# Experts' numbers cast on VectorE, each unit's weight loads listed whole, and the order behind the first stage searched anew

## The chip, the cores and the metric

The kernel runs on one core of one Trainium2 chip. The metric is the device time of one execution in microseconds (us), from launch to the last output. The core has five engines with a queue of instructions each: TensorE (PE; its weight loads are shown as PEld), VectorE (DVE), ScalarE (ACT), GpSimd (POOL) and SyncE (SP, which here only issues DMA transfers and reads registers). Each engine takes its instructions strictly in the order in which they are listed, and waits at each one until what it needs is there.

## The reference

Three layers follow each other, all in float32:

```
attention   q, k, v [4, 8, 768, 64]; chunks of 32 queries see 8 memory keys and 56 keys around them
            out[:, :, chunk] = softmax(q_c k_full^T / 8) v_full         -> x [3072, 512]
first MLP   h = x @ w_in [512, 2048];  g = h * tanh(softplus(h));  y = g @ w_out [2048, 512]
MoE         logits = normalized(y) @ normalized(expert_emb [8, 512]).T / tau
            expert_idx = argmax(logits);  gate_w = softmax(logits)[expert_idx]
            for e in 8:  out[rows of e] = gate_w * (relu(y[rows of e] @ w1[e]) @ w2[e])
                         w1[e] [512, 1024], w2[e] [1024, 512]
```

## The kernel before

**Stages.** The 24 pairs of attention blocks run first and beside the first MLP. The MLP is cut into 8 blocks of 384 rows and 16 slices of 128 of the 2048 columns: 128 steps. A step is 12 matmuls into `p_h` (L732), a chain of elementwise work that goes to and fro between ScalarE and VectorE (tanh, square, exp, `rn` on ScalarE; `m` L751 on VectorE; a square L755 on ScalarE; L758, L761 on VectorE; the cast `gh` L334; `gl` L769 on VectorE), and 9 matmuls into `p_y` (L778). Every float32 operand is split into a high and a low part, so that three matmuls stand for one.

**MoE.** Rows are sorted by expert into slots of 128 rows. A *unit* is one or two slots of one expert: units 0 to 2 (two slots each) come from the first 21 row tiles ("group 1" of the routing), units 3 to 15 (pairs and singles) need all 24 tiles ("group 2"). For each unit GpSimd gathers its rows (`vn`, L1288), TensorE turns them (`p_xT`, L1331), then come the matmuls with `w1` (`p_h`, L1395 for two slots, L1429 for one) and with `w2` (`p_y`, L1485), a scaled copy `yo` (L1505, L1507) and a scatter by GpSimd (L1511). The expert's weights, 4 MB, come in eight transfers `eraw` of 512 KB (L1314), issued by SyncE into one of two sets of buffers; each piece is split into `ehi` (a cast, L334) and `elo` (a difference, L1367) before TensorE can use it.

**Routing.** In each group TensorE first counts (L1035/L1036 in group 1, L1061 in group 2), VectorE works out from the counts each row's place and each unit's expert `ef` (L1144 to L1146) and whether it differs from that of two units before, `ci` (L1152, L1153), TensorE makes the table of row numbers `p_tab` (L1218), and VectorE copies it (L1230) and makes `gi` (L1232), by which GpSimd gathers. `ei` is `ef` as whole numbers: a cast of at most 20 numbers in one partition (L1175). SyncE reads a unit's expert from `ei` into a register before that unit's first weight load:

```
if c == 0 and second == 0:
    tl["ev", u] = nc.sync.value_load(ei[0:1, x:x + 1], min_val=0, max_val=NE - 1)
```

So no weight of a unit can be loaded before its group's cast L1175 is done. That cast was given to GpSimd, behind the group's first two gathers.

**What sets the order.** All work is put down as jobs with the engines that may do them, a cost in ns, a rank and the jobs they come after. `Plan.order()` goes through a planned time and gives each engine the ready job of lowest rank; the order that comes out is what is listed. A job's rank gets a correction from the table `NUDGE`, one number for each kind of job and stretch of the program, found by search. The chip sees only the order.

Of the kernel before, what the change touches and what calls it, by code (L numbers as in the profile page):

```python
# [86 lines left out]
def between(a, b):  # L87
# [12 lines left out]


NUDGE = dict(
    acta0=-0.6, acta1=-1.74, acta2=50.36, actb0=-1.76, actb1=-96.54, actb2=-81.79, actb3=-42.59, att00=40.88,
    att01=6.03, att02=-14.41, att03=12.63, att04=-3.12, att05=6.33, att06=-6.99, att07=-18.03, att10=10.46, att11=7.93,
    att12=-2.03, att13=-0.28, att14=-5.39, att15=28.34, att16=0.19, att17=-11.65, att20=7.04, att21=-2.49, att22=6.84,
    att23=0.68, att25=11.02, att26=-13.24, att27=2.06, att30=-0.41, att31=-70.31, att32=-0.58, att33=-1.39,
    att35=-0.38, att36=-1.67, att37=-67.52, att40=0.45, att41=-0.43, att42=13.06, att43=-2.17, att44=-38.4,
    att45=12.86, att46=9, att47=-2.37, att50=-1.08, att51=-18.11, att52=-6.46, att53=252.42, att54=-0.22, att55=-3.21,
    att56=-1.09, att57=2.56, att60=-5.29, att61=2.16, att63=-69, att64=-3.49, att65=145.06, att66=-0.33, att67=-14.14,
    att70=-0.37, att71=-329.92, att72=0.25, att73=-193.55, att74=-10.54, att75=-2.18, att76=-1.27, e00=-1.37, e01=8.52,  # L110
    e10=3.1, e11=23.17, e20=-86.99, e21=1, e30=0.07, e31=1.64, e40=10.43, e41=28.57, e50=1.56, e51=-2.1, e60=-22.39,
    e61=17.86, e70=-0.44, e71=-5.41, em=3.37, en0=24.71, en1=-0.52, en2=4.38, en3=27.95, en4=-27.14, en5=-7.94,
    hh0=0.33, hh1=-9.8, hh2=7.9, ld00=-15.25, ld01=24.83, ld10=34.53, ld11=33.12, load0=8.15, load1=17.34, load10=5.31,
    load2=-45.54, load3=-3.15, load4=-2.18, load5=-0.64, load7=3.07, load9=4.58, mm_y0=20.47, mm_y1=14.69, mm_y2=275.2,
    mm_y3=-0.5, out0False=-95.98, out0True=2.61, out1False=4.84, out2False=6.58, raw0=-8.26, raw1=5.15, raw10=24.34,
    raw11=134.61, raw2=-9.44, raw3=-3.37, raw4=-0.07, raw5=-13.38, raw6=29.5, raw7=26.79, raw9=-0.21, route=3.96,
    rows0=21.85, rows1=0.04, rows2=2.04, split0=0.59, split10=130.91, split11=-16.93, split3=-2.85, split4=-6.67,
    split5=17.18, split6=34, split9=27.54, xs0=0.9, xs1=0.33, xs2=-187.61, ye0=0.64, ye1=82.2, ye2=137.26, ye3=-2.03,
    ye4=8.94, ye5=-5.92, yre0=-32.64, yre1=-4.26, yre3=-2.85, yre4=22.58, yre5=-10.72,
)  # L120
ATT = dict(q=0, k1=0, k2=0, Tq=1, Tk=1, qT=1, kT=1, v=2, mem=2, mem0=2, S=3, mx=3, ex=4, rg=5, rc=5, norm=5, PT=6, pT=6, V=7, xh=7, xl=7)

# [1 line left out]
def part(key):  # L124

    if key[0] == "issue":
        key = key[1:]
    n = key[0]
    x = key[1] if len(key) > 1 and isinstance(key[1], int) else 0
    if n in ATT:  # L130
        return f"att{x if x < 3 else min(x // 3, 5) + 2}{ATT[n]}"
    if n == "load":
        return f"load{x if x < 8 else 8 + x // 8}"
    if n in ("sign", "bias", "high", "low"):
        return f"raw{x if x < 8 else 8 + x // 8}"
    if n in ("hi", "lo"):
        return f"split{x if x < 8 else 8 + x // 8}"
    if n == "mm_y":
        return f"mm_y{0 if x < 4 else 1 if x < 24 else 2 if x < 48 else 3}"
    if n in ("tanh", "sq", "exp", "rn", "m"):  # L140
        return f"acta{0 if x < 4 else 1 if x < 24 else 2 if x < 48 else 3}"
    if n in ("m2", "rr", "g", "gh", "gl"):
        return f"actb{0 if x < 4 else 1 if x < 24 else 2 if x < 48 else 3}"
    if n in ("yT", "yb1", "yr1", "yb2", "yb3", "yL", "yL2", "ysq"):
        return f"rows{0 if x < 6 else 1 if x < 21 else 2}"
    if n in ("yout", "ystore", "y0out", "y0store", "y0load"):
        return f"out{0 if x < 6 else 1 if x < 21 else 2}{n[1] == '0'}"
    if n in ("shi", "slo"):
        return f"e{min(x, 6) if x < 6 else 6 + x % 2}{key[2]}"
    if n in ("hhi", "hlo", "relu", "hT"):  # L150
        return f"hh{0 if x < 6 else 1 + x % 2}"
    if n in ("xT", "xsh", "xsl"):
        return f"xs{0 if x < 6 else 1 + x % 2}"
    if n == "ld":
        return f"ld{0 if x < 2 else 1}{key[2]}"
    if n in ("ye", "yre", "en"):
        return f"{n}{x}"
    if n == "em":
        return "em"
    if n in ("r", "ids", "cnt", "tab"):  # L160
        return "route"
    return None


class Plan:
# [5 lines left out]
    def job(self, key, fn, on, rank, after=(), get=(), use=(), lat=130, tiled=False, dmas=0):  # L171
        uses = list(use) + [h for _, h in get]
        for h in uses:
            self.users.setdefault(h, []).append(key)
        for _, h in get:
            self.getter[h] = key
        self.jobs[key] = dict(fn=fn, on=on, rank=rank + NUDGE.get(part(key), 0), after=list(after), get=list(get), use=list(use), lat=lat, tiled=tiled, dmas=dmas,
                              need=[(tag, sum(t == tag for t, _ in get)) for tag in dict(get)])
# [102 lines left out]
def attn_moe_moe_kernel(ctx, tc, q, k, v, mem_k, mem_v, w_in, w_out, emb, tau, w1, w2, cst, out, ydbg=None):  # L281
    nc = tc.nc
# [30 lines left out]
    job, A, V_, G, E = plan.job, "Activation", "DVE", "Pool", "PE"  # L313
# [603 lines left out]
    ef, ei, ci = const.tile([1, NUNIT], F32, name="ef"), const.tile([1, NUNIT], I32, name="ei"), const.tile([1, NUNIT], I32, name="ci")  # L917
# [10 lines left out]
    def routing():  # L928
# [8 lines left out]
        rank = {1: KFF * NBLK - 12, 2: KFF * NBLK - 9}  # L937
# [42 lines left out]
        def group(g):  # L980
            i0, i1 = (0, T1) if g == 1 else (T1, NTILE)
            n = i1 - i0
            S8, c = [128, n, NE], slice(i0, i1)
# [3 lines left out]
            rk = rank[g]  # L987
# [169 lines left out]
            if g == 1:  # L1157
                ex = steps(experts(0, u1, evens[1], "e1") + change(2, 0, u1 - 2), [k3], rk)
# [12 lines left out]
            first = 0 if g == 1 else u1  # L1171

            def numbers(e):
                c = slice(first, u1 if g == 1 else NUNIT)
                nc.gpsimd.tensor_copy(ei[:, c], ef[:, c])  # L1175

            job(("experts", g), numbers, {G: 200}, rank=rk, after=[ex] + [("issue", "gather", first, a) for a in range(2)])


            CH = 3 if g == 2 else CH1  # L1180
# [74 lines left out]

        plan.group = group
        group(1)
        group(2)

    NC_ = 4
# [4 lines left out]
    def unit(u, base, x, cols, main=True, after=0, then=0):  # L1267
# [3 lines left out]
        g = 1 if x < FIRST // 2 else 2  # L1271
# [4 lines left out]
        def put_job(key, fn, on, rank, after=(), get=(), use=(), dma=None):  # L1276
            if not main:
                fn(next(iter(on)))
            elif dma:
                plan.dma(key, fn, on, dma, rank, after, get, use)  # L1280
            else:
                job(key, fn, on, rank, after, get, use)
# [16 lines left out]
        def load(second, c):  # L1299
            def f(e):  # L1300
                if c == 0 and second == 0:
                    tl["ev", u] = nc.sync.value_load(ei[0:1, x:x + 1], min_val=0, max_val=NE - 1)
                    if main and u >= 2:
                        tl["cv", u] = nc.sync.value_load(ci[0:1, x:x + 1], min_val=0, max_val=1)
                if u < 2:
                    raw[b, second, c] = wp.tile([128, 1024], F32, tag=f"w{8 * b + 4 * second + c}", name="eraw")
                kw = dict(cond=tl["cv", u]) if main and u >= 2 else {}
                if second:
                    src = w2[bass.ds(tl["ev", u], 1), c * 256:(c + 1) * 256, :].rearrange("a (k p) f -> p (a k) f", p=128)
                    dst = raw[b, second, c].rearrange("p (k f) -> p k f", k=2)  # L1310
                else:
                    src = w1[bass.ds(tl["ev", u], 1), :, c * FC:(c + 1) * FC].rearrange("a (k p) f -> p (a k) f", p=128)
                    dst = raw[b, second, c].rearrange("p (k f) -> p k f", k=KDM)
                nc.sync.dma_start(out=dst, in_=src, **kw)  # L1314
            return f

        for second in range(2):
            for c in range(NC_):
                h = ("eraw", b, second, c)
                after = [("experts", g)] + ([("slo", u - 2, second, c)] if u >= 2 else [])  # L1320
                if c or second:
                    after.append(("issue", "ld", u, second, c - 1) if c else ("issue", "ld", u, 0, NC_ - 1))
                put_job(("ld", u, second, c), load(second, c), dict(SP=470), base - 7 + 1.5 * second + 0.3 * c, after,
                        [(f"w{8 * b + 4 * second + c}", h)] if u < 2 else [], [] if u < 2 else [h], dma=2 ** 19)


# [168 lines left out]
        for n in range(2 * NC_ if split_y else 0):  # L1495
            c = n % NC_
# [23 lines left out]
    def late(n, x, cols):  # L1520
        unit(FIRST // 2 + MAIN_P + MAIN_S + n, 0, x, cols, False)
# [70 lines left out]
    for kind, n in TURNS:  # L1592
        c = FIRST + 2 * n
        todo.append((FIRST // 2 + n, [c, c + 1]) if kind == "P" else (FIRST // 2 + PAIRS + n, [FIRST + 2 * PAIRS + n]))
    base = KFF * NBLK
# [51 lines left out]
```

## Time and profile before

| what | us |
|---|---|
| median of 3 runs (lowest, highest) | 1021.76 (1020.55, 1022.34) |
| the profiled execution's own time | 1021.15 |
| its span, first to last instruction | 1019.4 |
| TensorE busy | 991.5 (97%) |
| VectorE, ScalarE, GpSimd busy | 809.0, 648.8, 189.5 |
| mean granted TensorE clock | 0.991 of full speed |

TensorE is busy for 97% of the span, so the table says which engine bounds the kernel and how little idle time there is to take away, some 28 us. It does not say where that time lies, nor what is lost where TensorE is busy at a lower clock. Both are read from the stretches and waits that are shown below.

### The profile page before, as it was taken

Reading aid. Unit: us, or ns where it says so; the run is one execution under the profiler, and the core shown is the slowest. Engines: PE = TensorE matmul, PEld = TensorE weight load, DVE = VectorE, ACT = ScalarE, POOL = GpSimd, SP = SyncE. Lnnn points to the kernel's source line nnn. Section 1 sums busy time; section 2 is a strip of 40 time slices with the busy share of each in tenths; the row PEclk is TensorE's granted clock in tenths of the full one; section 3 lists DMA queues with packets and bytes.
Section 4 is the critical chain, followed back from the end, with each engine's and each line's share of the span. In section 5 each row is a group of like instructions: output and inputs, shape, how many; then the busy total and the mean of one; then the engine's idle time right before and its main releaser. Section 6 shows DMA issues by size and latency. Waiting matters only on the chain.

```text
span 1019.4 us, 22817 instructions
## 1 busy us (share of the span) xinstructions
PE 991.5 (97%) x8575; PEld 879.2 (86%) x8575; DVE 809.0 (79%) x1799; ACT 648.8 (64%) x1534; POOL 189.5 (19%) x142
## 2 busy tenths in 40 slices
PE   7899999999999999999999999999989999999997
PEld 6678888898888888888888899888979988988986
DVE  4889999669899869769869867979948667777972
ACT  4788888776877777778777767757424334443431
POOL 5000100000000000000000000011136455555742
PEclk9989999999999999999999999999989999999999
DMA  9997661233645234325313100089089868467300
GB/s 181 253 237 200 168 184 45 59 128 97 184 132 135 74 78 134 84 46 145 84 25 122 30 20 20 1 272 327 32 279 371 280 229 296 150 218 246 127 29 23
DMA packets 171817, 146.36 MB, mean 144 GB/s; under 512 B 105114, under 2 KB 134410, under 8 KB 171444
## 3 DMA queue, kind: packets, MB, share of 16 engines
q1 hardware_dynamic: 164868, 128.53, 43.5%
q0 software_dynamic: 5104, 15.89, 4.6%
q8 instruction: 69, 1.13, 0.5%
q10 hardware_dynamic: 1728, 0.43, 0.3%
q14 instruction: 48, 0.39, 0.1%
HBM read 137.11 MB, written 16.53 MB: 151 GB/s over the span
## 4 chain that ended last, share of the span: by engine, by line
PE 76%; DVE 8%; DMA 7%; issue 5%; POOL 2%; SPq 1%; ACT 0%; POOLq 0%; DVEq 0%
PE p_h L732 23%; PE p_y L778 23%; PE p_y L1485 10%; PE p_h L1395 9%; DMA eraw<-in_moe_w_dram 2%; PE p_h L1429 2%; DMA kn<-in_k_dram 2%; PE p_X L621 2%; PE p_S L559 2%; POOL elo L1367 1%; SPq L319 1%; PE p_PT L602 1%; PE p_xT L1331 1%; PE p_qT L511 1%; DMA qn<-in_q_dram 1%
## 5 line engine op out<-in xcount | busy, mean ns | idle before, releaser
L732 PE MATMUL p_h<-xt,win_h 128*128 128x384 f32 x1024 | 268.9, 344 | 0.6 <-DVE rn L761 0.5
L732 PEld LDWEIGHTS p_h<-xt,win_h 128*128 128x128 f32 x1024 | 185.3, 191 | 10.2 <-DVE rn L761 1.8
L732 PE MATMUL p_h<-xt,win_l 128*128 128x384 f32 x512 | 173.9, 340 | 0.0
L334 ACT CAST ehi<-eraw 128x1024 fp32r<-128x1024 f32 x89 | 92.9, 1049 | 120.0 <-PE p_y L1485 67.7
L778 PE MATMUL p_y<-wout_h,gh 128*128 128x512 f32 x384 | 157.1, 409 | 0.0
L778 PE MATMUL p_y<-wout_h,gl 128*128 128x512 f32 x384 | 151.9, 396 | 0.0
L778 PE MATMUL p_y<-wout_l,gh 128*128 128x512 f32 x384 | 151.8, 395 | 0.0
L1367 DVE TENSOR_TENSOR elo<-eraw,ehi 128x1024 fp32r<-128x1024 f32 x89 | 127.9, 1444 | 28.3 <-ACT ehi L334 27.7
L1485 PE MATMUL p_y<-ehi,hh 128*128 128x512 f32 x432 | 144.1, 400 | 0.0
L1395 PE MATMUL p_h<-xs,ehi 128*128 128x256 f32 x704 | 128.3, 283 | 7.0 <-DVE xs L1348 2.5
L755 ACT ACTIVATE m<-m,cf 128x384 f32<-128x384 f32 x128 | 79.1, 618 | 70.6 <-DVE m L751 69.7
L1395 PEld LDWEIGHTS p_h<-xs,ehi 128*128 128x128 f32 x704 | 110.4, 191 | 10.3 <-DVE xs L1348 2.7
L1367 POOL TENSOR_TENSOR elo<-eraw,ehi 128x1024 fp32r<-128x1024 f32 x39 | 94.9, 2432 | 81.1 <-DVE ehi L334 36.6
L851 DVE SCALAR_TENSOR_TENSOR junk<-ysb,en 128x512 f32<-128x512 f32 x144 | 99.0, 688 | 3.0 <-DMA ysb<-y_d 2.7
L1395 PE MATMUL p_h<-xs,elo 128*128 128x256 f32 x352 | 99.3, 282 | 0.0
L732 PEld LDWEIGHTS p_h<-xt,win_l 128*128 128x128 f32 x512 | 97.4, 190 | 0.0
L1485 PEld LDWEIGHTS p_y<-ehi,hh 128*128 128x128 f32 x432 | 80.9, 188 | 18.2 <-DVE hh L1454 0.3
L751 DVE SCALAR_TENSOR_TENSOR m<-sq,rn 128x384 f32<-128x384 f32 x128 | 71.0, 555 | 31.1 <-ACT rn L324 29.8
L758 DVE SCALAR_TENSOR_TENSOR rn<-m,rn 128x384 f32<-128x384 f32 x128 | 71.5, 558 | 30.0 <-ACT m L755 27.9
L736 ACT ACTIVATE sq<-p_h 128x384 f32<-128x384 f32 x128 | 62.8, 491 | 41.2 <-PE p_h L732 40.8
L778 PEld LDWEIGHTS p_y<-wout_h,gl 128*128 128x128 f32 x384 | 72.2, 188 | 17.3
L1485 PE MATMUL p_y<-elo,hh 128*128 128x512 f32 x216 | 85.2, 394 | 0.0
(264 smaller groups left out, 1770.8 us busy)
## 6 DMA issues: line engine op xcount, KB each, us to landing
eraw<-in_moe_w_dram SPq DMA_DIRECT2D x128, 512.0 KB
en<-en_d SPq DMA_DIRECT2D x48, 256.0 KB
vn<-in_v_dram SPq DMA_DIRECT2D x162, 56.0 KB
raw<-in_moe_w_in_dram SPq DMA_DIRECT2D x16, 512.0 KB
raw<-in_moe_w_out_dram SPq DMA_DIRECT2D x16, 512.0 KB
y_d<-ysb SPq DMA_DIRECT2D x24, 256.0 KB
qn<-in_q_dram SPq DMA_DIRECT2D x22, 256.0 KB
ysb<-y_d SPq DMA_DIRECT2D x18, 256.0 KB
```

What stands on the lines that cost most here:

```text
L334: (nc.scalar.copy if e == A else nc.vector.tensor_copy)(out, src)
L559: nc.tensor.matmul(ps[s][r:r + CHUNK, h, n // 2, :], a[64 * s:64 * s + 64, n, QB * h + CHUNK * x:QB * h + CHUNK * x + CHUNK], c[64 * s:64 ...
L732: nc.tensor.matmul(p, w, xt[j][:, a, kk, :], start=(n == 0), stop=(n == len(ops) - 1))
L736: nc.scalar.activation(t, tl["h", s], AF.Tanh, scale=0.5)
L751: nc.vector.scalar_tensor_tensor(t, tl["sq", s], 4.0, tl["rn", s], ALU.add, ALU.mult)
L755: nc.scalar.activation(t, t, AF.Square, bias=c15)
L758: nc.vector.scalar_tensor_tensor(tl["rn", s], tl["m", s], 0.75, tl["rn", s], ALU.add, ALU.mult)
L778: nc.tensor.matmul(yp[yh][t], x[:, c], w[g][:, o, :], start=(first and n == 0), stop=(final and n == 2))
L851: nc.vector.scalar_tensor_tensor(junk, tl["yio", t][:, 1], 1.0, tl["en", j, x], ALU.mult, ALU.mult, accum_out=lg[:, i, x:x + 1])
L1367: engs[e].tensor_sub(tl["elo", j], raw[b, second, c], tl["ehi", j].bitcast(F32))
L1395: nc.tensor.matmul(p[:, o, :], w[:, kk, s], v[:, kk, :], start=(kk == 0 and m == 0), stop=(kk == KDM - 1 and m == 2))
L1485: nc.tensor.matmul(tl["yy", u][a], v[:, kk, s], w[:, k, :], start=(kk == 0 and m == 0), stop=(kk == KEF - 1 and m == 2))
```

## The change

There are three edits.

1. The cast L1175 goes from GpSimd to VectorE, and no longer comes after the group's first two gathers: it comes after the last of the steps that make `ef` and `ci`. Its cost in the plan goes from 200 to 80 ns.
2. A unit's first weight load comes after the issue of the last one of the unit in front (`("issue", "ld", u - 1, 1, NC_ - 1)`), so that eight loads stand together; and the plan now counts 950 or 1450 ns more for a unit's first load, at which SyncE reads one or two registers.
3. `NUDGE` has new numbers for everything behind the first stage.

```diff
@@ numbers of the experts @@
             def numbers(e):
                 c = slice(first, u1 if g == 1 else NUNIT)
-                nc.gpsimd.tensor_copy(ei[:, c], ef[:, c])
-
-            job(("experts", g), numbers, {G: 200}, rank=rk, after=[ex] + [("issue", "gather", first, a) for a in range(2)])
+                nc.vector.tensor_copy(ei[:, c], ef[:, c])
+
+            job(("experts", g), numbers, {V_: 80}, rank=rk, after=[ex])
@@ loads of a unit @@
                 after = [("experts", g)] + ([("slo", u - 2, second, c)] if u >= 2 else [])
+                if u and c == 0 and second == 0:
+                    after.append(("issue", "ld", u - 1, 1, NC_ - 1))
                 if c or second:
                     after.append(("issue", "ld", u, second, c - 1) if c else ("issue", "ld", u, 0, NC_ - 1))
-                put_job(("ld", u, second, c), load(second, c), dict(SP=470), base - 7 + 1.5 * second + 0.3 * c, after,
+                put_job(("ld", u, second, c), load(second, c), dict(SP=470 + (0 if c or second else 950 if u < 2 else 1450)), base - 7 + 1.5 * second + 0.3 * c, after,
@@ NUDGE, one line of seventeen @@
-    acta0=-0.6, acta1=-1.74, acta2=50.36, actb0=-1.76, actb1=-96.54, actb2=-81.79, actb3=-42.59, att00=40.88,
+    acta0=-0.6, acta1=-1.74, acta2=87.07, acta3=0.02, actb0=-1.76, actb1=-96.54, actb2=-5.71, att00=40.88, att01=6.03,
```

The number of matmuls and of weight loads on TensorE is the same, and the order on every engine is the same up to about the fourteenth of the 128 steps. From line 1321 on a line of the kernel before stands two lines further down in the changed one (L1367 becomes L1369, L1348 becomes L1350, L1511 becomes L1513).

GpSimd's queue from the first gathers (`vn`) on, before the change; `ei` is the experts' numbers, the first cast that of group 1, the second that of group 2, and `out_dram` a scatter:

```order
L1288 DMA vn<-y_d,gi 128x512 x2
L1175 CAST ei<-ef 1x3
L1288 DMA vn<-y_d,gi 128x512 x4
L1511 DMA out_dram<-yo,si 3072x512 x4
L1288 DMA vn<-y_d,gi 128x512 x2
L1175 CAST ei<-ef 1x20
L1367 TENSOR_TENSOR elo<-eraw,ehi 128x1024
```

The second cast stands behind eight gathers and four scatters, those of units 0 and 1 and the gathers of unit 3. VectorE's queue in the changed kernel, at the place where group 2's table `p_tab` has been made:

```order
L1167 CAST ra<-ra 1x3
L1208 TENSOR_TENSOR rhs_9724<-rhs_9724,ra 128x3x32
L1230 COPY ra<-p_tab 128x96
L1175 CAST ei<-ef 1x20
L1369 TENSOR_TENSOR elo<-eraw,ehi 128x1024
L1231 SCALAR_TENSOR_TENSOR ra<-ra 128x32
L1350 TENSOR_TENSOR xs<-p_xT,xs 128x4x128
L1232 CAST gi<-ra 128x32
```

The same cast now stands right behind the copy of the table. SyncE's queue at the first weight loads, before the change (`ISA` rows set an address from the register):

```order
L940 DMA cf<-in_consts_dram 128x342
L1302 TENSOR_LOAD ei
L1302 ISA x2
L1314 ISA
L1314 DMA eraw<-in_moe_w_dram 128x4x256
L1302 TENSOR_LOAD ei
```

And in the changed kernel, the end of unit 0's loads:

```order
L1314 ISA
L1314 DMA eraw<-in_moe_w_dram 128x2x512
L1302 TENSOR_LOAD ei
L1302 ISA x2
L1314 ISA
L1314 DMA eraw<-in_moe_w_dram 128x4x256
```

Unit 1's first load stood behind unit 0's first, and the rest of the two units' loads went on in turn; now eight loads of unit 0 (four of 128x4x256, four of 128x2x512) stand ahead of it. VectorE's queue behind group 1's table work in the changed kernel:

```order
L1208 TENSOR_TENSOR rc<-rc,ra 128x6x6
L769 TENSOR_TENSOR gl<-rn,gh 128x384
L751 SCALAR_TENSOR_TENSOR m<-sq,rn 128x384
L758 SCALAR_TENSOR_TENSOR rn<-m,rn 128x384
L1230 COPY ra<-p_tab 128x18
L761 SCALAR_TENSOR_TENSOR rn<-rn,p_h 128x384
L1231 SCALAR_TENSOR_TENSOR ra<-ra 128x6
L334 CAST gh<-rn 128x384
L1232 CAST gi<-ra 128x6
L769 TENSOR_TENSOR gl<-rn,gh 128x384
```

The two `gl` are those of steps 118 and 119, whose nine matmuls each stand next to each other on TensorE, the first of them right behind the table. On TensorE, from the counts of group 1 to its first table, there stood 6 steps' `p_h` and 5 steps' `p_y` before and there stand 5 and 4 now; from the table of group 2 (24 matmuls) to the first `p_h` of unit 3 there stood 12 turns, 60 `p_y` and 96 `p_h` matmuls before, and there stand 16, 84 and 96 now.

## Rows read from the trace of the kernel before

**Rows 1.** TensorE's waits from 150 us on: us in total, times, longest.
```profile
PE p_h L1395 <- DVE xs L1348: 2.5, 1, 2.5
PE p_h L1395 <- ACT xs L334: 1.9, 1, 1.9
PE p_h L1395 <- DVE rn L761: 1.8, 1, 1.8
PE p_h L1395 <- DVE hh L1412: 0.7, 1, 0.7
PE p_xT L1331 <- DMA vn<-y_d,gi: 0.3, 1, 0.3
```

**Rows 2.** Stretches: length, busy of PE, PEld, DVE, ACT, POOL; PEclk, DMA share, GB/s.
```profile
110.00:640.00 530.00, 529.33 (x4723) 469.16 (x4724) 435.45 (x1098) 402.36 (x1038) 11.37 (x16) 1.00 0.33 92
637.70:660.88 23.18, 23.18 (x121) 21.00 (x120) 21.35 (x76) 15.99 (x32) 0.00 (x0) 1.00 0.00 1
...
110.30:113.70 3.40, 3.31 (x12) 3.35 (x13) 3.40 (x8) 2.49 (x6) 0.00 (x0) 0.50 0.81 237
680.33:690.00 9.67, 9.62 (x70) 9.00 (x71) 8.81 (x11) 7.86 (x10) 0.00 (x0) 1.00 1.06 371
758.80:765.60 6.80, 5.16 (x24) 5.16 (x25) 3.09 (x4) 1.30 (x2) 2.87 (x2) 0.50 1.04 389
```

**Rows 3.** TensorE in time order, 755 to 766 us: start, us, instruction, [idle before].
```profile
755.21 0.40 PE L1485 MATMUL p_y<-ehi,hh 128*128 128x512 f32 x1
757.51 0.38 PE L1395 MATMUL p_h<-xs,ehi 128*128 128x256 f32 x1 [1.90 <-ACT xs L334]
760.44 0.58 PE L1395 MATMUL p_h<-xs,ehi 128*128 128x256 f32 x1 [2.55 <-DVE xs L1348]
...
765.52 0.45 PE L1395 MATMUL p_h<-xs,ehi 128*128 128x256 f32 x2
```

**Rows 4.** The chain that ended last, 736 to 764 us: start, us, what.
```profile
737.38 2.67 POOL vn L1288
...
742.17 0.19 POOL ei L1175
...
743.83 3.40 DMA eraw<-in_moe_w_dram
...
749.92 9.15 DMA eraw<-in_moe_w_dram
```

**Rows 5.** ScalarE in time order, around 755 us.
```profile
755.44 1.04 ACT L334 CAST ehi<-eraw 128x1024 fp32r<-128x1024 f32 x1 [7.14 <-DMA eraw<-in_moe_w_dram]
```

**Rows 6.** VectorE in time order, 731 to 735 us.
```profile
731.50 0.16 DVE L1153 CAST ci<-ra 1x4 int32<-1x4 f32 x1
...
734.22 0.25 DVE L1230 COPY ra<-p_tab 128x96 f32<-128x96 f32 x1
```

**Rows 7.** TensorE in time order: the table of group 2.
```profile
727.78 1.19 PE L1218 MATMUL p_tab<-rhs,o 128*128 128x96 bf16 x24
```

**Rows 8.** The chain over the whole span: one step's matmuls, and 24 of L1485.
```profile
203.07 2.10 PE p_y L778 x9
...
865.48 5.60 PE p_y L1485 x24
```

**Rows 9.** ScalarE and VectorE in time order, ahead of 680 us.
```profile
676.82 1.05 ACT L334 CAST ehi<-eraw 128x1024 fp32r<-128x1024 f32 x1 [1.82 <-DMA eraw<-in_moe_w_dram]
```
```profile
677.90 1.23 DVE L1367 TENSOR_TENSOR elo<-eraw,ehi 128x1024 fp32r<-128x1024 f32 x1 [2.31 <-ACT ehi L334]
```

**Rows 10.** VectorE in time order, counts of group 1 to two steps' gl.
```profile
637.98 0.33 DVE L1046 COPY ra<-p_t 128x168 f32<-128x168 f32 x1 [0.57 <-PE p_t L1035]
...
658.00 0.14 DVE L1153 CAST ci<-ra 1x1 int32<-1x1 f32 x1
...
658.17 0.54 DVE L769 TENSOR_TENSOR gl<-rn,gh 128x384 fp32r<-128x384 f32 x1
...
662.52 0.56 DVE L769 TENSOR_TENSOR gl<-rn,gh 128x384 fp32r<-128x384 f32 x1
```

More of the change, by code (lines that the diff above doesn't have):

```diff
@@ L102 @@
 NUDGE = dict(
-    acta0=-0.6, acta1=-1.74, acta2=50.36, actb0=-1.76, actb1=-96.54, actb2=-81.79, actb3=-42.59, att00=40.88,
-    att01=6.03, att02=-14.41, att03=12.63, att04=-3.12, att05=6.33, att06=-6.99, att07=-18.03, att10=10.46, att11=7.93,
+    acta0=-0.6, acta1=-1.74, acta2=87.07, acta3=0.02, actb0=-1.76, actb1=-96.54, actb2=-5.71, att00=40.88, att01=6.03,
+    att02=-14.41, att03=12.63, att04=-3.12, att05=6.33, att06=-6.99, att07=-18.03, att10=10.46, att11=7.93,
     att12=-2.03, att13=-0.28, att14=-5.39, att15=28.34, att16=0.19, att17=-11.65, att20=7.04, att21=-2.49, att22=6.84,
@@ L107 @@
     att35=-0.38, att36=-1.67, att37=-67.52, att40=0.45, att41=-0.43, att42=13.06, att43=-2.17, att44=-38.4,
[L108 to L116, printed above, removed]
@@ L117 @@
-    rows0=21.85, rows1=0.04, rows2=2.04, split0=0.59, split10=130.91, split11=-16.93, split3=-2.85, split4=-6.67,
-    split5=17.18, split6=34, split9=27.54, xs0=0.9, xs1=0.33, xs2=-187.61, ye0=0.64, ye1=82.2, ye2=137.26, ye3=-2.03,
-    ye4=8.94, ye5=-5.92, yre0=-32.64, yre1=-4.26, yre3=-2.85, yre4=22.58, yre5=-10.72,
+    att45=12.86, att46=9, att47=-2.37, att50=-1.08, att51=-18.11, att52=-6.46, att53=177.42, att54=-31.18, att55=30.31,
+    att56=187.87, att57=-0.62, att60=-115.93, att61=32.95, att62=53.76, att63=-28.94, att64=-129.86, att65=178.59,
@@ new lines @@
+    att66=-260.71, att67=-3.85, att70=6.83, att71=-116.86, att72=35.91, att73=-58.9, att74=0.86, att75=-1.81,
+    att76=-3.47, att77=-1.11, e00=0.14, e01=-111.3, e10=66.65, e11=-3.74, e20=213.28, e21=-0.44, e31=0.66, e40=2.22,
+    e41=1.95, e50=69.1, e51=-0.06, e60=0.27, e61=-3.93, e70=-10.23, e71=115.3, em=-84.23, en1=-185.31, en2=0.46,
+    en4=8.72, en5=-0.48, hh1=-8.45, hh2=-11.28, ld01=-39.06, ld10=12.21, ld11=0.34, load0=8.15, load1=17.34,
+    load10=5.31, load2=-45.54, load3=-3.15, load4=-2.18, load5=-0.64, load7=3.07, load9=4.58, mm_y0=20.47, mm_y1=14.69,
@@ new lines @@
+    mm_y2=228.49, mm_y3=-0.3, out0False=-3.7, out0True=2.61, out1False=-2.73, out2False=-115.98, raw0=-8.26, raw1=5.15,
+    raw10=24.34, raw11=-2.06, raw2=-9.44, raw3=-3.37, raw4=-0.07, raw5=-13.38, raw6=29.5, raw7=26.79, raw9=-0.21,
+    route=-0.07, rows1=-191.57, rows2=-70.31, split0=0.59, split10=130.91, split11=-9.16, split3=-2.85, split4=-6.67,
+    split5=17.18, split6=34, split9=27.54, xs0=-1.46, xs1=-0.39, xs2=-140.94, ye0=8.3, ye1=172.68, ye2=88.41,
+    ye3=-10.46, ye4=-9.41, ye5=-0.42, yre0=16.24, yre1=-168.75, yre2=-13.67, yre3=-38.98, yre4=0.81,
```

## The prediction

> **What bounds the kernel now.** I read the page first: TensorE is busy for 97% of the span, so time can only come out of its waits or out of stretches in which its clock is low. The windows came next: the reader is to see that the 530 us from 110 to 640 hold 529.33 us of TensorE's work at a clock of 1.00 [rows 2]. Most of the 128 steps lie there, and nothing can be taken away; the new order there can only keep that or lose. Then TensorE's waits behind 150 us: five entries make 7.3 us, and three of them 6.2 us [rows 1]. In time order two of these three stand in one place, the start of unit 3: TensorE ends unit 2 at 755.61, waits 1.90 us, does one group of `p_h`, waits 2.55 us and goes on at 760.44 [rows 3], at half the clock until the row of 765.52 [rows 2, 3]. The third, 1.78 us, ends at 680.33, where unit 0 starts, and no low clock follows it [rows 2].
>
> **Why unit 3 is late.** I followed the chain of work back from 760.44. ScalarE's cast `ehi` at 755.44 had waited 7.14 us for a weight load [rows 5], and the `xs` for which TensorE waits stand behind it in ScalarE's queue. That load landed after 9.15 us of DMA from 749.92, the first of its unit had gone out at 743.83, and ahead of it stood the cast `ei` on GpSimd at 742.17, behind a gather that had begun at 737.38 [rows 4]. `ef` and `ci` were ready far earlier: the cast `ci` had run at 731.50 [rows 6]. So some ten microseconds go by in which the number is known but GpSimd gathers and scatters.
>
> **The cast on VectorE.** It stands right behind `ra<-p_tab` in the new order. The table was made on TensorE from 727.78 to 728.97 [rows 7]; VectorE came to the copy at 734.22 [rows 6]. No trace shows the cast on VectorE. At best it ends 1 us behind the table, at worst, if VectorE is as late as now, at 734.47, or 5.5 us behind it. Its own cost is like that of `ci`, 0.16 us, where 3.40 us and more of other work of VectorE's lies beside TensorE's; I cost it at nothing. From the cast at 742.17 to `p_h` going at 760.44 it took 18.3 us [rows 3, 4], made of register reads, loads, split and `xs`. I leave that as it is, so `p_h` of unit 3 can go 19.3 to 23.8 us behind the table. TensorE gets there, without waiting, 26.6 us behind the table now (755.61 less 728.97), and in the new order 24 matmuls of `p_y` more stand between, 5.60 us [rows 8], so 32.2 us. The margin is 8.4 to 12.9 us: both waits go, **−4.45 us**. With them goes the low clock. From 760.44 to 765.52 it ran at half, and half of 5.08 us is **−2.54 us**.
>
> Next late behind this would be unit 3's rows: `gi` needs the same table, and GpSimd's first gather of the unit stood right ahead of the old cast, so it does not get later; I give it no price.
>
> **Loads listed whole.** Unit 0's wait of 1.78 us is for `rn` (L761) of an MLP step, which frees a PSUM buffer. VectorE was late with it: its `elo` at 677.90 had waited 2.31 us for `ehi`, and that 1.82 us for a weight load [rows 9]. Loads of units 0 and 1 went out in turn there, so that each unit got half the transfers. With unit 0's eight together its pieces land in half the time from the first one on, and the new order lists group 1's routing about one step of three earlier against the MLP. So the wait goes, **−1.78 us**; at worst it stays. A later read of `ei` or `ci` by SyncE now holds up nothing but the loads of its own unit. For units from 3 on the two sets of buffers are free at other times, but all loads are done ahead of need, except at the places named; nothing is added.
>
> **What the new order puts at risk around group 1.** From the counts to the first table TensorE now has 5 `p_h` and 4 `p_y` steps, nine blocks of 2.10 to 2.11 us [rows 8], where there were eleven, 23.18 us [rows 2]. VectorE must, from the counts at 637.98 to `gl` of that stretch at 658.17, do the routing and the steps: 20.19 us for 70 instructions [rows 10], 20 of them MLP ones. The new order has 82 to the same point, 11 of them MLP ones. Below: nine MLP ones fewer at the 0.54 us of `gl`, 21 small ones more at the 0.14 of `ci` [rows 10], 20.19 − 4.86 + 2.94 = 18.3 us, in time against 19.0 + 0.5 for nine blocks and the table. Above: 82 at the mean of all, 21.35/76 = 0.28 us [rows 2], 23.0 us, 3.5 late. Behind it two `p_y` steps stand next to each other; their `gl` come at least one chain apart, 4.35 us now (658.17 to 662.52 [rows 10]), and TensorE has one block of 2.10 between, so up to 2.25 us more. The ends are 0 and 5.7 us. MLP work was cut most, and the small instructions are nearer to the lower end, so I take **+1.5 us**.
>
> **The middle.** The new order of the steps from 150 us on cannot be priced from any row of before; the nearest is 0.67 us idle in 530 us [rows 2], and the bounds are 0 and about 3 us, five waits of the size 0.7 in [rows 1]. I take **+0.8 us**. The small waits in the units (0.7 and 0.3 [rows 1]) I leave where they are. Pieces of work handed between GpSimd, VectorE and ScalarE lie beside a TensorE that is full; they cost nothing unless a `gl` comes late, which is the rival below.
>
> **Sum.** The profiled execution took 1021.15 us, span 1019.4: 1021.15 − 4.45 − 2.54 − 1.78 + 1.5 + 0.8 = 1014.7. The median is 0.61 above the profiled one: **1015.3 us**. The likeliest case's own range, from no new wait at all but 0.3 us (1013.3, and 0.8 lower if the small waits of the units go too) to 2.7 us more of them, is 1012.5 to 1018.
>
> **Rivals.** (1) *A new wait costs the clock too.* At 110.3 a wait of 1.36 us was followed by 3.40 us at 0.50 [rows 2]; at 758.8 the waits of 1.90 and 2.55 by 6.80; behind the 1.78 us at 680.33 the clock stayed at 1.00 [rows 2]. So it can go either way. If the waits around group 1's table are 3 us and more, with two low stretches of 3.4 us that cost half each, +3.4: 1018.7. The Trainium skill says, in "TensorE: Matmul & The Clock Gate", section "HAM oscillation — how this bites in real kernels", that when TensorE is starved between groups of matmuls the clock falls back and the next group starts slow, each time anew. The trace agrees at 758.8 and at 110.3, and not at 680.33; by that rule the 1.78 us at 680.33 would have been followed by a slow group too, and its removal would be worth more than I count.
>
> (2) *The wait of unit 3 is not the cast's.* If what is late is a load or VectorE's split, and not the number, all of the first term stays: 1021.76 − 1.78 + 1.5 + 0.8 = 1022.3, no change. Against it: 7.14 us of waiting at that `ehi`, and the load issued right behind the cast's register read [rows 4, 5].
>
> (3) *Slower: the new order of the steps makes VectorE or ScalarE late with `gl`, step after step.* In steps with attention work between, TensorE comes back to a step's `p_y` only a few blocks behind its `p_h`. A lateness of 0.1 us in some 100 steps is 10 us. For the kernel to end above 1023.8 it takes 8.5 us more than the sum has; at 0.11 us a step it comes to 1026. For it: nothing in the trace tells what a chain in another order takes. Against it: VectorE has 435 us of work in those 530, ScalarE 402, and with that slack TensorE stood still for 0.67 us in all [rows 2].
>
> (4) *Nothing new goes wrong*, 0 to +0.3 in place of 2.3, and the small waits in the units shrink: 1012 to 1013.
>
> **How the numbers follow.** My forecast .60, (1) .13, (2) .10, (3) .10, (4) .07. A measurement of this kernel tells 0.2% from no change, about 2 us, so the bounds are 1019.7 and 1023.8. Forecast, (1) and (4) are faster, .80; (2) is the same, .10; (3) slower, .10. The range is 1011 to 1021: down past (4) by the spread of the runs, up past (1); it leaves out (2) and (3), 2 in 10.
>
> **What would show it.** Right, step by step: the first load of unit 3 goes out within 8 us of group 2's table; no wait of TensorE over 0.5 us at unit 3's first `p_h` and no stretch at 0.50 there; none for `rn` L761 at unit 0. One or two waits of 0.5 to 3 us for `gl` L769 at the two steps behind group 1's table. TensorE still busy for over 526 of the 530 us from 110 on. Wrong: the table's copy or the counts reach VectorE so late that the cast has lost its lead; a new stretch at half the clock; waits for `gl` or `rn` strewn over the steps.

## The result and the profile after

The changed kernel takes 1011.36 us (median of 4 runs, 1011.29 to 1011.48), the kernel before 1021.15 us (median of 4 runs, 1019.84 to 1022.34). The ratio is 0.9905, 95% interval 0.9887 to 0.9922: 9.8 us faster. Forecast were 6.5 us, 1015.3 us with a range of 1011 to 1021; the measured time lies inside that range by 0.4 us, and below the 1012.5 to 1018 that the forecast called likeliest. The profiled execution took 1011.35 us, its span is 1009.5 us.

The page's first line of the changed kernel, busy time by engine:

```profile
PE 987.1 (98%) x8575; PEld 875.7 (87%) x8575; DVE 788.9 (78%) x1799; ACT 654.7 (65%) x1545; POOL 186.2 (18%) x131
```

TensorE's waits from 150 us on in the changed kernel, to be read against [rows 1]:

```profile
PE p_xT L1333 <- DMA vn<-y_d,gi: 0.9, 1, 0.9
PE p_h L732 <- DVE rn L761: 0.4, 1, 0.4
```

Of the five waits of before only one for a gather is left, at another place and longer (0.9 us for 0.3), and one small wait in the middle is new. 7.3 us have become 1.3. Stretches of the changed kernel (columns as in [rows 2]): the middle; group 1 from its counts to `gl`; unit 0's start; unit 3's start; and behind the wait at 110 us:

```profile
111.40:640.00 528.60, 528.20 (x4726) 468.01 (x4727) 434.80 (x1131) 408.33 (x1048) 5.62 (x6) 1.00 0.34 92
622.90:641.90 19.00, 19.00 (x113) 17.21 (x111) 18.85 (x85) 12.38 (x24) 0.00 (x0) 1.00 0.00 1
752.60:759.40 6.80, 6.80 (x57) 6.66 (x57) 3.85 (x5) 3.67 (x5) 2.34 (x2) 1.00 1.07 363
673.00:683.00 10.00, 10.00 (x76) 9.50 (x75) 7.72 (x12) 5.52 (x8) 0.52 (x1) 1.00 0.80 255
...
111.31:114.71 3.40, 3.40 (x80) 3.10 (x80) 3.39 (x8) 2.50 (x7) 0.00 (x0) 1.00 0.89 249
```

TensorE is full in each of the places on which the prediction set a price, and its clock is 1.00 there. The last line is a surprise: at the same place, behind a wait of the same length (1.4 us for VectorE's `kT`), the kernel before ran 3.40 us at 0.50 [rows 2]. The order of instructions there is the same in both kernels.

VectorE in time order in the changed kernel, group 1's counts and the two `gl`, then group 2's copy and cast, and under it SyncE's first load of unit 3:

```profile
623.30 0.33 DVE L1046 COPY ra<-p_t 128x168 f32<-128x168 f32 x1
...
641.20 0.54 DVE L769 TENSOR_TENSOR gl<-rn,gh 128x384 fp32r<-128x384 f32 x1
...
644.47 0.56 DVE L769 TENSOR_TENSOR gl<-rn,gh 128x384 fp32r<-128x384 f32 x1
...
721.27 0.24 DVE L1230 COPY ra<-p_tab 128x96 f32<-128x96 f32 x1
721.43 0.15 DVE L1175 CAST ei<-ef 1x20 int32<-1x20 f32 x1
```
```profile
723.06 3.42 SPq L1314 DMA_DIRECT2D eraw<-in_moe_w_dram  x5
```

From the counts to `gl` VectorE took 17.9 us, against 20.19 before [rows 10]; the second `gl` follows 3.27 us behind the first, against 4.35. Group 2's table was done at 720.6 us. The cast ended 1 us behind it and the first load went out 2.5 us behind it; before, that load went out 14.9 us behind the table [rows 4, 7].

So the span fell by 9.9 us. Waits behind 150 us gave 6.1 (those of 0.1 and 0.2 us included), the low stretch at unit 3 gave 2.5, the one at 110 us gave 1.7 (half of 3.40). That is 0.4 us more than was measured. In the first stage, whose order is the same, the changed kernel was 0.9 us later at the wait for `kT` (it ends at 111.31 us, before at 110.39); the other 0.5 us, gained behind it, is in none of these rows.

### The profile page after: what moved, and what is told of

The parts are those of the page before. It is cut to its first block, busy times and chain, and to the rows that moved or that the text cites. A ratio compares the mean times of both kernels' runs of the same rounds, so it can differ in the third digit from the quotient of the medians.

```text
span 1009.5 us, 22854 instructions
## 1 busy us (share of the span) xinstructions
PE 987.1 (98%) x8575; PEld 875.7 (87%) x8575; DVE 788.9 (78%) x1799; ACT 654.7 (65%) x1545; POOL 186.2 (18%) x131
## 5 line engine op out<-in xcount | busy, mean ns | idle before, releaser
L1369 DVE TENSOR_TENSOR elo<-eraw,ehi 128x1024 fp32r<-128x1024 f32 x89 | 118.8, 1343 | 26.8 <-ACT ehi L334 25.5
L1397 PE MATMUL p_h<-xs,ehi 128*128 128x256 f32 x704 | 125.2, 279 | 0.0
L1369 POOL TENSOR_TENSOR elo<-eraw,ehi 128x1024 fp32r<-128x1024 f32 x39 | 93.7, 2403 | 81.5 <-ACT ehi L334 38.5
L1288 POOL DMA_INDIRECT vn<-y_d,gi x27 | 31.8, 1177 | 360.6 <-DMA eraw<-in_moe_w_dram 304.6
```

The source lines that it names most:

```text
L1288: nc.gpsimd.indirect_dma_start(out=tl["xg", u, a], out_offset=None, in_=y_d[0:T1 * 128, :] if g == 1 else y_d[:, :], in_offset=bass.Indire ...
L1369: engs[e].tensor_sub(tl["elo", j], raw[b, second, c], tl["ehi", j].bitcast(F32))
L1397: nc.tensor.matmul(p[:, o, :], w[:, kk, s], v[:, kk, :], start=(kk == 0 and m == 0), stop=(kk == KDM - 1 and m == 2))
```

## The experiments

In each of them the order that the plan gives is kept on every engine, and single instructions are moved in it, so that one edit is seen without a new search. Four or fewer kernels share one chip with runs of the kernel before, whose medians there were 1020.1, 1021.9 and 1021.2 us. In each sitting times spread by some us (the kernel before 1018.3 to 1025.0 in the first), so differences under about 2 us are read from waits in the profile and not from medians.

**1. Group 2's cast alone, in the old order.**

```diff
-GpSimd, behind unit 3's first two gathers:   ei<-ef 1x20
+VectorE, behind ra<-p_tab 128x96 (L1230):    ei<-ef 1x20
```

> The kernel before with one instruction moved: group 2's cast of the experts' numbers runs on VectorE right behind the copy of the table, and nothing else changes its place on any engine. Theory (the number's wait on GpSimd makes unit 3 late): the first load of unit 3 goes out at about 736 us instead of 743.8, some 7.7 us earlier, which is more than the 4.45 us that TensorE waits there. Both waits at unit 3 go, and the stretch at half the clock with them: 1021.2 - 4.45 - 2.54 = 1014.2 us. The 1.78 us at unit 0 stay. Rival (what is late at unit 3 is the transfers or VectorE's own queue, not the number): the waits stay within 1 us of what they are, 1020 to 1021 us.

Measured: 1014.59 us, ratio 0.9936 (0.9920 to 0.9953). TensorE's longest waits from 150 us on, and under them the stretch behind unit 0's wait:

```profile
PE p_h L1395 <- DVE rn L761: 1.9, 1, 1.9
PE p_h L1395 <- DVE hh L1412: 0.3, 1, 0.3
```
```profile
681.30:684.70 3.40, 3.40 (x18) 3.40 (x17) 3.12 (x4) 2.87 (x4) 0.00 (x0) 0.51 1.10 360
```

Both waits of unit 3 are gone and unit 0's is still there, as the theory had it, and the time is within 0.4 us of its 1014.2. The cast by itself is enough to take unit 3's waits away in the old order. Unit 0's wait, of nearly the same length as before, was this time followed by a low stretch.

**2. Whole loads alone, in the old order.**

```diff
-SyncE: unit 0 and 1's loads in turns, unit 3 and 4's too, some of units 9 to 15
+SyncE: eight loads of a unit, then eight of the next
```

> The kernel before with only SyncE's weight loads in another order: each unit's eight whole, behind those of the unit in front; both casts stay on GpSimd. Theory of the prediction: the wait of 1.78 us at unit 0 goes and nothing else does, 1019.4 us. Rival A (the taking of turns is what makes unit 3 late as well, since the transfers of units 3 and 4 share the queue): the 4.45 us at unit 3 shrink too, by up to all of it and of the 2.54 us of low clock, 1012.4 to 1017 us. Rival B (unit 0's wait has another cause than the turns): no change, 1021 us.

Measured: 1019.19 us, ratio 0.9982 (0.9966 to 0.9999); the profiled execution took 1016.0. TensorE's longest waits from 150 us on; then one row each of VectorE, ScalarE and TensorE in time order; then the stretch behind TensorE's wait:

```profile
PE p_h L1395 <- DVE hh L1412: 4.4, 1, 4.4
PE p_h L1395 <- DVE xs L1348: 0.6, 1, 0.6
```
```profile
675.83 0.55 DVE L761 SCALAR_TENSOR_TENSOR rn<-rn,p_h 128x384 f32<-128x384 f32 x1
```
```profile
684.86 1.99 ACT L334 CAST ehi<-eraw 128x1024 fp32r<-128x1024 f32 x2 [7.59 <-DMA eraw<-in_moe_w_dram]
```
```profile
688.96 0.80 PE L1395 MATMUL p_h<-xs,ehi 128*128 128x256 f32 x2 [4.43 <-DVE hh L1412]
```
```profile
688.96:692.36 3.40, 3.40 (x16) 3.40 (x17) 3.40 (x5) 3.40 (x5) 0.00 (x0) 0.50 1.05 385
```

My theory holds for the wait it was about: the 1.78 us for `rn` are gone, VectorE ends that `rn` at 676.38 and TensorE goes past it at 676.53. But nothing is gained by it, for some 8 us later TensorE waits 4.43 us at another `p_h` of unit 0, for `hh`, and a low stretch follows. ScalarE's list there has a cast of unit 1's weights between those of unit 0, as the turns would bring them. With whole loads unit 1's first piece comes behind all of unit 0's, ScalarE stood still for 7.59 us, and what unit 0 needs stood behind. At unit 3, of which I had expected nothing, 4.45 us of waits fell to 0.6 and the low stretch went (rival A). The turns of units 3 and 4 were a second cause of that wait: to remove either one is enough, or nearly.

**3. Both casts and whole loads, in the old order.**

```diff
+both casts on VectorE, as in experiments 1 and 9
+whole loads, as in experiment 2
```

> The kernel before with both casts on VectorE (group 1's right behind the last step that makes the numbers, group 2's right behind the copy of the table) and each unit's loads whole, the order of everything else as before. If the first two edits make the gain and the new order adds nothing of its own: 1021.2 - 4.45 - 2.54 - 1.78 = 1012.4 us, within 1 us of the changed kernel's 1011.4 (the rest is one low stretch of 1.7 us at 110 us and 0.7 us of small waits). If the new order is needed for it: 1015 us or more, with waits left at units 0 or 3.

Measured: 1015.56 us, ratio 0.9953 (0.9934 to 0.9971), so 4.8 of the 9.8 us. TensorE's waits from 150 us on, and two rows of the chain that ended last, around 660 us:

```profile
PE p_xT L1331 <- DMA vn<-y_d,gi: 3.1, 2, 2.9
PE p_h L732 <- DVE rn L761: 0.9, 3, 0.5
```
```profile
660.49 4.05 DMA eraw<-in_moe_w_dram
...
664.69 7.02 DMA vn<-y_d,gi
```

Neither unit 0's nor unit 3's `p_h` waits, but a new wait is there: unit 0's gather, issued at 664.69 behind weight loads that had begun at 660, took 7.02 us to land, and TensorE stood at `p_xT` for 2.9 us. So in the old order the first two edits together (0.47%) gain no more than group 2's cast by itself did in experiment 1 (0.64%; the two intervals overlap).

**4. Group 2's cast given back to GpSimd, in the new order.**

```diff
-VectorE, behind ra<-p_tab 128x96:            ei<-ef 1x20
+GpSimd, behind unit 3's first two gathers:   ei<-ef 1x20
```

> The changed kernel with group 2's cast given back to GpSimd, behind the first two gathers of unit 3; nothing else moves. In the changed kernel these gathers end at 727.6 us and the number would be there some 6.2 us later than it is now. Theory by the prediction's margin (p_h of unit 3 can go 18.3 us behind the cast, and TensorE comes to it 32.5 us behind the table): 7.2 + 18.3 = 25.5 us, so no wait at unit 3's p_h; at most ScalarE, which has a cast of unit 3's weights listed ahead of a yo of unit 2, holds TensorE up for 0 to 3 us: 1011.4 to 1014.5 us. Rival (the cast's place is worth the 7 us by itself, in any order): 1016 to 1018.5 us.

Measured: 1011.19 us, ratio 0.9900 (0.9883 to 0.9917). TensorE's waits from 150 us on, then GpSimd's cast and SyncE's first loads of unit 3 in time order:

```profile
PE p_xT L1333 <- DMA vn<-y_d,gi: 0.9, 2, 0.6
PE p_h L732 <- DVE rn L761: 0.2, 1, 0.2
```
```profile
729.87 5.89 POOL L1175 CAST ei<-ef 1x20 int32<-1x20 f32 x1
```
```profile
737.24 1.07 SPq L1314 DMA_DIRECT2D eraw<-in_moe_w_dram  x2
```

Counted from the gathers, the cast starts 6.2 us later than in the changed kernel (2.85 us ahead of the first there, 3.34 behind its start here). It also took 5.89 us, for a reason that no row shows (0.19 in the kernel before), and SyncE read the number right behind its end. So the first load went out 14.3 us behind the table (at 722.94), nearly as late as before the change (14.9), and still TensorE did not wait for it at unit 3's `p_h`. In the new order with whole loads unit 3 has the slack (24 more matmuls stand in front of its `p_h`, and experiment 2 showed what whole loads do there); the move of this cast is worth nothing there.

**5. Group 1's cast given back, in the new order.**

```diff
-VectorE, behind ci<-ra (L1153):              ei<-ef 1x3
+GpSimd, behind unit 0's first two gathers:   ei<-ef 1x3
```

> The changed kernel with group 1's cast given back to GpSimd, behind the first two gathers of unit 0; group 2's cast stays on VectorE and nothing else moves. Theory A (in the new order the place of group 1's cast matters): the gathers end at 647.8 us, so unit 0's first load goes out at about 649.5 instead of 641.9 us and lands 7 us later, at about 653 us; ScalarE has the first cast of these weights listed at 646.5 us, in the middle of the MLP's last steps, and stands still for some 6 us; TensorE then waits 3 to 6 us for gl or rn of those steps: 1014.5 to 1017.5 us. Theory B (there is slack for it, as there was for group 2's): 1011 to 1012 us.

Measured: 1018.49 us, ratio 0.9971 (0.9955 to 0.9988), 7 us slower than the changed kernel. One row of ScalarE in time order, then TensorE's longest wait, then the stretch about that wait's end:

```profile
653.21 1.04 ACT L334 CAST ehi<-eraw 128x1024 fp32r<-128x1024 f32 x1 [7.01 <-DMA eraw<-in_moe_w_dram]
```
```profile
PE p_y L778 <- ACT gh L334: 5.5, 1, 5.5
```
```profile
652.10:658.90 6.80, 4.09 (x9) 2.79 (x10) 3.78 (x8) 4.94 (x10) 0.00 (x0) 0.50 1.01 345
```

Theory A holds; the time lies 1 us above its range, which counts the wait and not the low stretch of 6.8 us, worth some 2 us (half of 4.09). The new order puts unit 0's first weight cast into the last MLP steps, and ScalarE waits there 7.01 us in front of a step's `gh`. Here the edit does its work: the early number of group 1 lets the new order be what it is.

**6. Units 0 and 1 in turns again, in the new order.**

```diff
-SyncE: eight loads of unit 0, then eight of unit 1
+SyncE: w1 of units 0 and 1 in turns, then w2 of each
```

> The changed kernel with the loads of units 0 and 1 taking turns again, as before the change; both casts on VectorE, nothing else moves. By the prediction (the turns made unit 0's wait of 1.78 us): the wait comes back, 1013.2 us. By what the kernel before with whole loads showed (the wait at unit 0 grew from 1.78 to 4.43 us, because ScalarE's casts there are listed in the order of the turns): in the new order the casts of unit 0 are listed whole, so with turns its third to eighth pieces come up to 7 us later than now. But the loads go out from 641.9 us on and unit 0's first p_h comes at 673.4: 31 us for 16 loads. So nothing at unit 0's p_h; 1011 to 1012 us.

Measured: 1012.58 us, ratio 0.9914 (0.9894 to 0.9935), the changed kernel's within the interval. TensorE's only wait from 150 us on:

```profile
PE p_h L732 <- DVE rn L761: 0.4, 1, 0.4
```

No wait at unit 0. Where the number of group 1 is early, the new order needs no whole loads there. (In the kernel before, too, only the `w1` loads of the two units took turns, four of each, and their `w2` loads stood whole, as here.)

**7. The new order alone.**

```diff
+both casts on GpSimd behind their group's first two gathers
+SyncE: all loads in the turns of the kernel before
```

> The changed kernel's new order without the first two edits: both casts on GpSimd behind the first two gathers of their group, the weight loads in the turns of the kernel before. If the new order by itself makes the gain (as group 2's cast given back, which cost nothing, suggests): within 1 us of the changed kernel, 1011 to 1012.5 us. If it was found around the early cast of group 1: ScalarE waits for unit 0's first weights in the middle of the last MLP steps as with that cast alone given back, and with turns the second piece comes later still: 1015 to 1020 us, though unit 3 has no wait.

Measured: 1022.96 us, ratio 1.0012 (0.9993 to 1.0031), above both ranges: the new order without the edits is worth nothing. TensorE's longest waits from 150 us on, and two stretches:

```profile
PE p_y L778 <- ACT gh L334: 4.5, 1, 4.5
PE p_h L1397 <- ACT xs L334: 1.3, 1, 1.3
PE p_h L732 <- DVE rn L761: 1.1, 1, 1.1
```
```profile
702.82:706.22 3.40, 3.40 (x16) 3.21 (x16) 2.08 (x6) 2.26 (x6) 1.01 (x2) 0.50 0.02 5
767.67:771.07 3.40, 3.40 (x17) 3.40 (x18) 3.05 (x3) 1.80 (x3) 2.95 (x3) 0.50 1.05 387
```

The first wait is that of experiment 5. The second is unit 3's, back in part and with a low stretch behind it (the second line): the late cast alone did not bring it back in this order (experiment 4), the late cast with the turns does, with the first load again 14.3 us behind the table. The first line is a low stretch with no wait ahead of it, to which the last section comes back.

**8. An attempt at a faster version.**

```diff
+VectorE:  rn L758, rn L761, kT, and then sp L374, win_l L404, which stood ahead of them
+ScalarE:  m L755, and then the cast of wout_h, which stood ahead of it
```

> A version that might beat the changed one. TensorE's longest wait that is no transfer is now 1.38 us at 109.9 us, before p_PT, for VectorE's copy kT, which stands behind sp, win_l and rn; and the p_h behind it waits for rn L761. Here VectorE does rn L758, L761 and kT first and sp and win_l (1.1 us) behind them, and ScalarE's cast of wout_h goes behind its square m. kT can then be done at 110.5 instead of 111.2 us: the wait falls to 0.6 us, the kernel to 1010.6 us, and no low stretch of the clock follows it. Rival: the pieces of weights put off make a later step wait, no change or slower.

Measured: 1010.71 us, ratio 0.9891 (0.9867 to 0.9915); the interval holds the changed kernel's 0.9905. TensorE's waits from 105 to 113 us:

```profile
PE p_k L511 <- ACT sq L736: 0.9, 1, 0.9
PE p_PT L602 <- DVE kT L334: 0.7, 1, 0.7
```

The wait for `kT` fell from 1.4 to 0.7 us as worked out, and a new one of 0.9 us came up in front of it. The rival is nearer: nothing gained that can be told from the changed kernel.

**9. Group 1's cast alone, in the old order.**

```diff
-GpSimd, behind unit 0's first two gathers:   ei<-ef 1x3
+VectorE, behind ci<-ra (L1153):              ei<-ef 1x3
```

> The kernel before with group 1's cast alone on VectorE, right behind the last step that makes the numbers; group 2's cast stays on GpSimd, the loads keep their turns. Theory (in the old order the early cast removes unit 0's wait for weights but sets 512 KB weight loads ahead of unit 0's gathers, which then take 7 us to land instead of 3.6 and keep TensorE waiting at p_xT, as with both casts and whole loads): 1.78 us go, some 2.9 us come, the 4.45 us at unit 3 and its low stretch stay: 1021 to 1022.5 us. Rival (the slow gather came of whole loads, not of the early cast): no wait at p_xT, unit 0's wait gone, 1019.4 us.

Measured: 1021.77 us, ratio 1.0006 (0.9990 to 1.0023). TensorE's longest waits from 150 us on, its first `p_xT` in time order, and the stretch behind that wait:

```profile
PE p_xT L1331 <- DMA vn<-y_d,gi: 3.4, 2, 2.9
PE p_h L1395 <- DVE xs L1348: 2.4, 1, 2.4
PE p_h L1395 <- ACT xs L334: 1.5, 1, 1.5
```
```profile
670.79 0.63 PE L1331 MATMUL p_xT<-cf,vn 128*128 128x128 f32 x4 [2.87 <-DMA vn<-y_d,gi]
```
```profile
670.79:677.60 6.81, 6.81 (x37) 6.02 (x38) 6.11 (x12) 3.16 (x6) 1.89 (x2) 1.00 1.07 367
```

The theory holds. The early cast removes unit 0's wait of 1.78 us, with the loads in turns, and it costs 2.87 us at the gather. That TensorE comes later does not explain why the wait for `rn` is gone: `rn` is done 8.8 us behind unit 0's first `p_xT` here and 10.0 in experiment 2, 11.9 before, and TensorE needs it 10.2 us behind. In its old place, behind the gathers, the cast had kept the weight loads from getting in front of them: unit 0's first gather landed 3.5 to 3.7 us after its issue in experiments 1, 2, 5 and 7, with the late cast, and 6.8 to 8.1 in the changed kernel and experiments 3, 4, 8, 9 and 10, with the early one.

**10. The changed kernel once more**, with no edit.

> The changed kernel once more, beside the others on one chip. By the result it takes 1011.4 us. The point is the clock: TensorE has the same wait of about 1.37 us at 110 us in every kernel here, and behind it a low stretch of 3.4 us in some profiles and none in others. If the low stretch hung on the order of instructions, this profile would again have none there; if it is chance, it may have one, and the time differs by 1.7 us.

Measured: 1011.92 us (1007.72 to 1013.60), ratio 0.9896 (0.9872 to 0.9920). Three stretches of its profile, and TensorE's rows ahead of the third:

```profile
110.90:114.30 3.40, 3.40 (x80) 3.10 (x80) 3.39 (x8) 2.50 (x7) 0.00 (x0) 1.00 0.83 245
690.20:693.60 3.40, 3.40 (x32) 3.31 (x31) 1.05 (x4) 3.31 (x10) 0.00 (x0) 1.00 0.56 161
693.60:697.00 3.40, 3.40 (x14) 2.91 (x13) 3.23 (x10) 2.84 (x5) 2.20 (x2) 0.51 0.19 54
```
```profile
689.33 1.47 PE L839 MATMUL p_yT<-cf,ysb 128*128 128x128 f32 x12
690.65 2.85 PE L860 MATMUL p_lg<-cf,yt 128*128 128x8 f32 x24
693.36 1.69 PE L1333 MATMUL p_xT<-cf,vn 128*128 128x128 f32 x8
```

No low stretch at 110 us again, but one at 693.6 that the first profile of the same kernel does not have.

## Why the prediction was right, and where it was not

**The cast on VectorE, −4.45 and −2.54: right in size and in the old order right in cause.** The number comes 1 us behind the table, the best end of the bounds, both waits are gone and the clock stays at 1.00. Experiment 1 gives it by itself. But I had taken one cause for the only one. Experiment 2 shows a second, the turns of units 3 and 4, and experiment 4 shows that in the new order with whole loads the cast's place is worth nothing at group 2. Part of that could be read from the prediction: the 5.60 us of matmuls that the new order sets in front of unit 3 are more than the whole wait of 4.45 us, and I only added them to the margin. They are not enough alone: with the late cast and the turns 1.6 us of waits are back there (experiment 7: 1.28 and 0.34). That the sum with one cause to each wait came out near was luck; the gains do not add up in that way.

**Loads listed whole, −1.78: right in size, half right in cause.** Whole loads do take away that wait by themselves (experiment 2). Two things failed. The step gave whole loads no price, and in the old order they bring a wait of 4.43 us at unit 0, since ScalarE's casts are still listed in the order of the turns. And it took the turns for the only cause: the early number of group 1 takes the wait away too, with the turns left as they are (experiment 9), and in the new order turns cost nothing (experiment 6). That early cast I had not priced at all, and it pays only with an order in which the gathers have time: in the changed kernel TensorE comes to unit 0's `p_xT` 12.5 us behind the gather's start (645.37 and 657.89 us), in the old order 4.1 us. Which of the many places that the new order moves are needed for this was not tested one by one. (Unit 0's first `p_h` began at 675.56; at 680.33, where the prediction has unit 0 start, the wait ends inside it.)

**Around group 1, +1.5: mis-sized.** It cost nothing. VectorE took 17.9 us for the 82 instructions, just below my lower end of 18.3, in time for the 19.5 that TensorE has; and the second `gl`, 3.27 us behind the first, was not waited for either (TensorE waited 0.12 us there, for the `gh` ahead of it). I had seen that the lower end was nearer and still took 1.5.

**The middle, +0.8: near.** One wait of 0.40 us, in 528.6 us without another; before 0.67 us were idle in 530 [rows 2]. The nearest row was the right guide.

**The clock.** 1.7 us of the profile's gain is the low stretch at 110 us, which no term of mine had and which the change did not touch. Without it and with the two positive terms at their measured 0 and 0.2, and with 0.1 us less of small waits in the units, the sum on the forecast's scale is 1021.76 − 8.77 + 0.2 − 0.1 = 1013.1, and 1011.4 with it. That it meets 1011.36 so closely is luck: the 0.61 us by which I set the median above the profiled run are gone with the result's fourth run (median 1021.15), and on the profile's scale the same sum gives 1010.8, 0.6 us under the profiled 1011.35. How many of the timed runs of either kernel had that low stretch is not known, so it explains the profile's difference and not surely the median's.

Rival 1 asked for new waits, and in the changed kernel there were none to test it on. (Its 1018.7 adds the low stretches alone to the forecast, which holds 1.5 us of waits there and not the 3 of its condition; with those it is 1020.2.) In the experiments the waits of 4.4 to 5.5 us (2, 5 and 7) all came with a low stretch. Of the shorter ones some did, as the 1.9 us in experiment 1 and the 1.3 us at unit 3 in experiment 7, and some did not, as the 2.9 us at `p_xT` in experiments 3 and 9. The Trainium skill, "TensorE: Matmul & The Clock Gate", section "HAM oscillation — how this bites in real kernels", has a starved TensorE start each next group slowly, in an example with waits of some 3 to 5 us. The rows agree where the waits were as long as that, 4.4 us and more; for shorter waits they agree in experiment 1 and not in the kernel before at 680.33 [rows 2], where the wait was nearly as long and at the same place.

**The rivals.** Rival 2 (unit 3's wait not the number's) is refuted as put, by experiment 1; what it named, a late load, was a second cause. Rival 3 (lateness in every step) is refuted by the middle's line. Rival 4 (nothing new goes wrong) is what happened; the time is 0.6 us under its 1012 to 1013, and without the low stretch at 110 us it would be at its upper end.

## What to carry to other kernels

A wait can have two causes of which removing either is enough: its price may then be booked to neither edit alone, and each is tested in the old order and in the new. Here the edits and the new order gain 9.8 us together; the new order alone gains nothing, and the edits without it half; group 2's cast alone, in the old order, gains two thirds (experiment 1). In the new order group 1's cast is what cannot be taken back (experiment 5); group 2's cast or the whole loads of units 0 and 1 can, one at a time (experiments 4 and 6). Before a transfer is allowed to start earlier, look for what had been held ahead of it by the old place: here two gathers, the first of which took 7.0 us behind weight loads and some 3.6 without them.

## What the runs showed of the hardware

TensorE's clock fell to its lower level (1.2 of 2.4 GHz, 0.50 in the rows) from case to case at the same place. Ten profiles have the same wait of 1.35 to 1.38 us at 108 to 113 us with the same work around it; behind it three ran 3.40 us at 0.50 (the kernel before, experiments 4 and 5) and seven did not. And a wait is not needed: in experiments 4, 6, 7 and 10 a low stretch of 3.4 us begins at 691 to 703 us with TensorE busy for all of the 3.40 us ahead of it, at or near the end of 24 matmuls of 128x8 (2.85 us) that follow 12 of 128x128; in the other three profiles of the new order (the changed kernel's first, experiments 5 and 8) the same rows ran on at 1.00. What decides it is not shown. Each such stretch is 1.7 us, so single profiles of one kernel differ by as much without any other cause.
